# Attention, routed experts and a second MLP on one core: pairs of token groups taken in the order 2, 0, 1 in hidden quarters two to four, and the first pair's plain operands read where they lie

## The chip, the core and the metric

The kernel runs on one core of one Trainium2 chip. The metric is the device time of one execution in microseconds (us), as the median of several runs. The core has five engines with their own instruction queues, each of which runs its instructions in the order of the program: TensorE (PE, matmuls; PEld is its loading of weights), VectorE (DVE), ScalarE (ACT), GpSimd (POOL) and SyncE (SP, which here only starts transfers). An instruction may wait for another engine or for a transfer, and all that stands behind it in its queue then waits too. Matmuls read SBUF and write PSUM; a transfer that POOL starts goes through one queue, one that SP starts through another, and both move on the same 16 DMA engines.

## The reference, cut to what matters

```python
x = attention(q, k, v, omega)        # 4 x 8 heads x 576 tokens, random features; 2304 rows of 512
x = moe(x, w_gate, w1, w2)           # each row to one of 8 experts, 512 -> 1024 -> 512

def _moe2_ref(x, w_in, w_out):       # 2304 rows, 512 -> 2048 -> 512
    h = x @ w_in
    neg, pos = h <= -1, h >= 1
    g = np.where(pos, h, np.where(neg, 0.0, (h + 1) ** 2 / 4))
    return g @ w_out
```

The change lies in the last part, `_moe2_ref`, here called the second MLP.

## The kernel before

**Precision.** Every fp32 operand of a matmul is split into a high part (rounded) and a low part (the rest). One product is then three matmuls: high by high, high by low, low by high. So each operand, weights and activations alike, costs one rounding copy (on ACT) and one subtraction (on POOL or DVE).

**Second MLP, tiling.** The 2304 rows, transposed, lie in SBUF as `yT` (four tiles of 128 features). They are taken in six groups g of 384 rows; the groups 2p and 2p+1 are the pair p (0, 1, 2). The 2048 hidden features are taken in quarters qd of 512, four blocks f of 128 each.

Quarter 0 runs over groups with plain products. `z_h(u, fs)` makes two hidden blocks of group u (24 matmuls), `z_o(0, u, fs)` multiplies two of them by w_out (18 matmuls); the order of work for group u is z_h(u, blocks 0 and 1), z_o(0, u-1, blocks 2 and 3), z_h(u, blocks 2 and 3), z_o(0, u, blocks 0 and 1). The high and low parts of group u lie in `ys[u % 2]`, made by `z_split` one group ahead. After each hidden block DVE and ACT alternate: DVE clips the bank (`z_clip`), ACT squares, DVE takes a maximum (`z_g`), ACT rounds, DVE subtracts (`z_low`). ACT also copies finished output banks to `st` before the next z_o may use them.

Quarters 1 to 3 run over pairs with a 2 by 2 scheme of seven products instead of eight. `s_h(qd, p, a)` makes, for one half a of the quarter, four hidden blocks of a pair from seven products of 6 matmuls each (42 in all; here called a set). Product i multiplies a weight combination by operand i of the pair, which lies in DRAM as `yd[p][i]` (768 KB). Operands 0, 4 and 6 are plain parts of x, which `y_keep` stores from `ys`; 1, 2, 3 and 5 are differences, which the step stream "y" makes during quarter 0 (DVE subtracts, `y_round` rounds on ACT, subtracts on POOL and stores). `y_load(k)` fetches operand k of the running list (seven for each pair, three pairs for each quarter) into slot k modulo 9 of `yslots`, from POOL's queue; in the second half of each set, product i is followed by the fetch of list entry `k0 + 9 + i`. A set's first product goes to bank b1, from which ACT copies it (x1); the fifth product is then added into b1. The sets use a ring of five PSUM banks (`ps_h2`), the output products one of three (`ps_o`).

**The order of the side work** is written out by hand. Three step streams ("w": read, convert, combine and round the weights of the next quarter; "y": the differences; "z": `z_split` of the next group) are advanced by `tick`; in quarter 0 the table `BEAT` says after each third of a matmul block which stream goes on (z, y, w, or h for `y_round`). `gate` holds the weight stream back until the weights it overwrites are no longer needed. The nine slots are the two halves of `ys[0]`, five parts of a tile `yS` that takes the place of `yT` once that is no longer read, and the two halves of `ys[1]`.

Of the kernel before, what the change touches and what calls it, by code (L numbers as in the profile page):

```python
# [19 lines left out]
P = 128  # L20
# [6 lines left out]
G = 384  # L27
# [134 lines left out]
def kernel(  # L162
# [1102 lines left out]
    half_ys = [t[:, i * 4 * G:i * 4 * G + 4 * G] for t in ys for i in range(2)]  # L1265
    yslots = half_ys[0:2]

    def y_slots():
        flat = yp.tile([P, 3 * YW], F32R, name="yS", tag="yT")
        yslots.extend([flat[:, i * 4 * G:(i + 1) * 4 * G] for i in range(5)] + half_ys[2:4])  # L1270
        flat = yp.tile([P, YW], F32, name="yW", tag="yT3")
        wz[2:] = [flat[:, i * 512:i * 512 + 512] for i in range(2)]
        sts[0] = flat[:, 1024:1024 + TG * D]
    ends = range(NTILE - 2 * TG, NTILE)
    sts = [None, zp.tile([P, TG * D], F32, name="st1", tag="st1", bufs=1)]
# [33 lines left out]
    def z_g(ph, cl, key):  # L1309
        qd, g, f = key  # L1310
        gt = gs[g % 2][f + 4 * ((3 * qd + g // 2) % 2) if g % 2 and f < 2 else f]
        gtiles[key] = gt[:, 0], gt[:, 1]
        nc.vector.tensor_tensor(out=cl, in0=ph, in1=cl, op=ALU.max)  # L1313
        nc.scalar.activation(gt[:, 0], cl, AF.Copy)  # L1314
        return gt, cl
# [30 lines left out]
    def z_o(qd, g, fs):  # L1346
# [28 lines left out]
        if qd == 0:  # L1375
            nc.sync.dma_start(out=zd[g], in_=z_stage(qd, g))
        elif qd < 3:
            nc.gpsimd.dma_start(out=zd[g], in_=z_stage(qd, g), accum_op=ALU.add)
        elif g + 2 < NG:
            z_fetch(g + 2)  # L1380

# [28 lines left out]
    def y_stream():  # L1410
        for p in range(NG // 2):
            for s in range(2):
                b11, b12, b21, b22 = [yT[2 * i + s][:, (2 * p + j) * G:(2 * p + j) * G + G] for i in range(2) for j in range(2)]
                t1 = None
                for op in (3, 1, 5, 2):
                    yield "D"
                    hi, t, both = pair()
                    x, y = {3: (b12, b11), 2: (b22, b12), 1: (b22, t1), 5: (t1, b21)}[op]
                    nc.vector.tensor_sub(t, x, y)
                    if op in (3, 1):  # L1420
                        t1 = t
                    high.append((p, op, s, hi, t, both))

    def z_stream(u):
        for d in range(4):
            yield "A"
            z_split(u, d, nc.gpsimd)

# [3 lines left out]
    def beat(u):  # L1432
        n = count[u] + 3 * (u == 0 and count[u] > 7)
        count[u] += 1
        name = BEAT[n]
        if u == 0:
            name = name if n < 19 and name == "z" else "w" if n >= 19 else None
        elif u == NG - 1 and n < 11 and name == "y":
            name = "w"
        if name == "h":  # L1440
            y_round()
        elif name:
            tick(name)

    def y_load(k):
        q, op = divmod(k, 7)
        if q < 9:
            nc.gpsimd.dma_start(out=yslots[k % NSL], in_=yd[q % 3][op])


    def s_h(qd, p, a):
        k0 = 7 * (3 * (qd - 1) + p)
        b1, b2, b3, b4 = [ps_h2.tile([P, 512], F32, name="ph2", tag="ph2")[:, 0:G] for _ in range(4)]

# [13 lines left out]
        product(0, b1, True)  # L1468
        nc.scalar.activation(x1, b1, AF.Copy)
        tick("w")  # L1470
        product(1, b2, True)
        if a and p == 2:
            gate[0] = qd + 1
# [7 lines left out]
        tick("w", "A")  # L1481
        product(4, b1, False)
        q11 = z_clip(b1)
        product(5, b2, True)
        nc.vector.tensor_sub(x2, x2, b2)
        l11 = z_g(*q11, (qd, g0, f0))
        q21 = z_clip(x2)
        product(6, b4, False)
        nc.vector.tensor_add(x1, x1, b4)
        z_low(*l11)  # L1490
        q22 = z_clip(x3, x4)
# [9 lines left out]
    for u in range(NG):  # L1501
# [3 lines left out]
        else:  # L1505
# [3 lines left out]
            y_slots()  # L1509
            for k in range(2, 7):  # L1510
                y_load(k)
# [6 lines left out]
        if u < NG - 1:  # L1518
            drain("z")
        if u == NG - 2:  # L1520
            y_load(0)
            y_load(1)
        z_o(0, u, (0, 1))
# [3 lines left out]
    for qd in range(1, 4):  # L1527
        if qd == 3:
            z_fetch(0)
        for p in range(3):  # L1530
            s_h(qd, p, 0)
            if (qd, p) == (1, 0):
                z_o(0, g, (2, 3))
            else:
                z_o(qd - (p == 0), g, (0, 1))
                z_o(qd - (p == 0), g, (2, 3))
            if p == 0:
                gate[1] = qd + 1
            if (qd, p) == (3, 0):
                z_fetch(1)  # L1540
            s_h(qd, p, 1)
            if (qd, p) == (3, 2):
                flat = yp.tile([P, 3 * YW], F32, name="yF", tag="yT")
# [3 lines left out]
            z_o(qd, g, (0, 1))  # L1547
            if (qd, p) == (1, 0):
                tick("w")
                tick("w")  # L1550
# [6 lines left out]
    tot = nc.values_load(ints[0:1, 3, 0:1], min_val=0, max_val=8 * 16)  # L1557
    last = [z_stage(3, g)[:, j * D:j * D + D] for g in (NG - 2, NG - 1) for j in range(TG)]
    fw = [yT[j // 10][:, j % 10 * 256:j % 10 * 256 + 256] for j in range(16)]
# [108 lines left out]
```

## Time and profile before

| | |
|---|---|
| time, median of 3 runs | 799.04 us (798.63 to 799.64) |
| profiled execution, its own time | 803.65 us |
| its span, first to last instruction | 801.9 us |
| PE busy in the span | 754.3 us (94%) |
| DVE, ACT, POOL busy | 550.9, 392.7, 378.7 us |
| mean granted TensorE clock | 0.978 |

The span is what the profile shows of one execution. 1.75 us of that execution's time lie outside it, and it was 4.6 us longer than the median of the timed runs. The granted clock is the share of TensorE's full speed; 0.50 is the lower of its two levels. In the views below a time in brackets, as [2.53 <-DMA yS<-yd], is how long the engine was idle just before the row, and what ended that.

### The profile page before, as it was taken

The page shows a single profiled execution, that of the slowest core. Times are in us where ns is not written, and L with a number is a line of the kernel's source. Part 1 is how long each engine was busy: PE and PEld are TensorE (multiplying, and loading weights), DVE is VectorE, ACT ScalarE, POOL GpSimd, SP SyncE. Part 2 cuts the span into 40 slices and gives each one's busy share as a digit, 9 for nine tenths or more (in the row PEclk, how much of TensorE's full clock was granted, in tenths as well). Part 3 has the DMA queues.
Part 4 walks back from the last instruction along what each step waited for, and adds up shares of the span by engine and source line. Part 5 has one row for each costly group of instructions (what it writes and reads, how often), then busy time and mean ns, then how long its engine had stood idle before and what let it go on. Part 6 is the DMA issues. An engine that isn't in the chain of part 4 may idle for free. (4 is left out here: it accounts for less than half of the span.)

```text
span 801.9 us, 17043 instructions
## 1 busy us (share of the span) xinstructions
PE 754.3 (94%) x6428; PEld 690.5 (86%) x6428; DVE 550.9 (69%) x1170; ACT 392.7 (49%) x973; POOL 378.7 (47%) x429
## 2 busy tenths in 40 slices
PE   6898899588999999999999999799999999999997
PEld 4787788558999999999989889589899889988985
DVE  3678787945756775565778887677656866676663
ACT  5999799522422222222356754354554554552230
POOL 5658851535455545523747876143145233432312
PEclk9999999888999999999999999799999999999999
DMA  9977301164566766655446588796987986968822
GB/s 220 228 162 220 94 30 29 72 181 158 174 198 196 216 183 219 211 171 159 132 140 263 236 318 295 297 384 168 314 273 190 376 247 196 358 195 306 307 112 83
DMA packets 94236, 166.61 MB, mean 208 GB/s; under 512 B 28528, under 2 KB 61424, under 8 KB 94144
## 3 DMA queue, kind: packets, MB, share of 16 engines
q1 hardware_dynamic: 79136, 93.91, 37.4%
q0 software_dynamic: 14112, 69.80, 26.8%
q10 hardware_dynamic: 896, 1.70, 0.6%
q8 instruction: 53, 0.87, 0.4%
q14 instruction: 39, 0.32, 0.1%
HBM read 125.29 MB, written 40.11 MB: 206 GB/s over the span
## 5 line engine op out<-in xcount | busy, mean ns | idle before, releaser
L278 POOL TENSOR_SCALAR wh<-wraw 128x1024 fp32r<-128x1024 f32 x60 | 73.1, 1219 | 106.7 <-DMA wraw<-in_moe_w_dram 69.0
L1357 PE MATMUL po<-wl,g 128*128 128x512 f32 x288 | 114.2, 397 | 1.4 <-POOL wl L300 1.4
L1356 PE MATMUL po<-wh,g 128*128 128x512 f32 x288 | 114.3, 397 | 1.3 <-ACT st L1362 1.3
L1358 PE MATMUL po<-wh,g 128*128 128x512 f32 x288 | 114.2, 396 | 0.0
L390 DVE TENSOR_TENSOR wl<-wraw,wh 128x1024 fp32r<-128x1024 f32 x60 | 85.3, 1430 | 9.5 <-POOL wh L278 9.5
L300 POOL TENSOR_TENSOR wl<-wz,wh 128x256 fp32r<-128x256 f32 (+1 forms) x43 | 40.4, 945 | 97.6 <-ACT wh L314 97.6
L616 ACT ACTIVATE pp<-ps,bi 128x128 f32<-128x128 f32 x288 | 84.5, 481 | 3.1 <-DVE bi L612 3.1
L1306 ACT ACTIVATE cl<-cl,half 128x384 f32<-128x384 f32 x78 | 47.4, 609 | 72.8 <-DVE cl L1305 72.8
L1156 PE MATMUL ph<-xh,wh 128*128 128x288 f32 (+6 forms) x256 | 77.9, 304 | 4.2 <-DVE hl L1162 3.8
L1157 PE MATMUL ph<-xl,wh 128*128 128x288 f32 (+6 forms) x256 | 77.7, 304 | 0.1
L1158 PE MATMUL ph<-xh,wl 128*128 128x288 f32 (+6 forms) x256 | 77.6, 303 | 0.0
L1174 PE MATMUL py<-hh,wh 128*128 128x288 f32 (+6 forms) x256 | 77.6, 303 | 0.0
L1176 PE MATMUL py<-hh,wl 128*128 128x288 f32 (+6 forms) x256 | 76.5, 299 | 0.0
L1175 PE MATMUL py<-hl,wh 128*128 128x288 f32 (+6 forms) x256 | 76.4, 298 | 0.0
L1357 PEld LDWEIGHTS po<-wl,g 128*128 128x128 f32 x288 | 54.5, 189 | 13.5 <-POOL wl L300 1.9
L1356 PEld LDWEIGHTS po<-wh,g 128*128 128x128 f32 x288 | 54.7, 190 | 13.1 <-ACT st L1362 1.6
L1358 PEld LDWEIGHTS po<-wh,g 128*128 128x128 f32 x288 | 54.5, 189 | 12.8
L1161 ACT ACTIVATE hh<-ph 128x288 fp32r<-128x288 f32 (+6 forms) x64 | 26.8, 418 | 76.3 <-PE ph L1158 74.1
L1318 DVE TENSOR_TENSOR g<-cl,g 128x384 fp32r<-128x384 f32 x78 | 48.3, 619 | 22.4 <-ACT g L1314 22.4
L1162 DVE SCALAR_TENSOR_TENSOR hl<-ph,hh 128x288 fp32r<-128x288 f32 (+6 forms) x64 | 29.1, 461 | 49.7 <-ACT hh L1161 49.6
L1314 ACT ACTIVATE g<-cl 128x384 fp32r<-128x384 f32 x78 | 40.5, 520 | 34.0 <-DVE cl L1313 33.9
L605 DVE TENSOR_REDUCE nsq<-ps 128x4 f32<-128x512 f32 x72 | 46.9, 683 | 11.5 <-PE ps L600 11.4
(218 smaller groups left out, 2078.0 us busy)
## 6 DMA issues: line engine op xcount, KB each, us to landing
wraw<-in_moe_w_dram SPq DMA_DIRECT2D x57, 512.0 KB, 4.0
yS<-yd POOLq DMA_DIRECT2D x35, 768.0 KB, 12.1
ys<-yd POOLq DMA_DIRECT2D x28, 768.0 KB, 12.5
yd<-tt SPq DMA_DIRECT2D x24, 384.0 KB, 2.6
wraw<-in_moe_w_in_dram SPq DMA_DIRECT2D x16, 512.0 KB, 6.7
wraw<-in_moe_w_out_dram SPq DMA_DIRECT2D x16, 512.0 KB, 8.2
yd<-ys SPq DMA_DIRECT2D x9, 768.0 KB, 5.3
zd<-st SPq DMA_DIRECT2D x6, 768.0 KB, 4.4
```

The lines of the kernel that those rows point to most:

```text
L278: nc.gpsimd.tensor_scalar(out=hi, in0=t, scalar1=1.0, scalar2=1.0, op0=ALU.mult, op1=ALU.mult)
L390: nc.vector.tensor_sub(lo, t, hi.bitcast(F32))
L616: act.activation(at(ppb)[:, 2 * j + i, :], at(pjb[i])[:, j, :], AF.Exp, bias=r["bi"][:, j, i:i + 1])
L1156: nc.tensor.matmul(ph, lhsT=wh[:, d, c], rhs=xh, start=(d == 0), stop=False)
L1157: nc.tensor.matmul(ph, lhsT=wh[:, d, c], rhs=xl, start=False, stop=False)
L1158: nc.tensor.matmul(ph, lhsT=wl[:, d, c], rhs=xh, start=False, stop=(d == 3))
L1174: nc.tensor.matmul(py, lhsT=wh[:, a, c], rhs=hh, start=(f == 0), stop=False)
L1175: nc.tensor.matmul(py, lhsT=wh[:, a, c], rhs=hl, start=False, stop=False)
L1176: nc.tensor.matmul(py, lhsT=wl[:, a, c], rhs=hh, start=False, stop=(f == 7))
L1356: nc.tensor.matmul(po, lhsT=gh[:, c], rhs=wh, start=(f == 0), stop=False)
L1357: nc.tensor.matmul(po, lhsT=gh[:, c], rhs=wl, start=False, stop=False)
L1358: nc.tensor.matmul(po, lhsT=gl[:, c], rhs=wh, start=False, stop=(f == 3))
```

## The change

Five things change together. Pairs are taken in the order 2, 0, 1 in quarters 1 to 3, and by the stream "y". The first nine slots are arranged so that the plain operands 0, 4 and 6 of pair 2 are read from `ys`, where groups 4 and 5 still lie; no transfer fetches them. In the two halves of that first set the products run in the order 0, 6, 4, 1, 2, 3, 5, product 6 into a fifth bank of its own that DVE adds later. `z_split` subtracts on DVE for the first two of its four parts, where POOL did all. In group 0 the weight stream gets two ticks that were empty.

```diff
-    yslots = half_ys[0:2]
+    ORDER = (2, 0, 1)
+    yslots = []
 
     def y_slots():
         flat = yp.tile([P, 3 * YW], F32R, name="yS", tag="yT")
-        yslots.extend([flat[:, i * 4 * G:(i + 1) * 4 * G] for i in range(5)] + half_ys[2:4])
+        part = [flat[:, i * 4 * G:(i + 1) * 4 * G] for i in range(5)]
+        yslots.extend([half_ys[0], part[0], part[1], part[2], half_ys[1], part[3], half_ys[3], part[4], half_ys[2]])
...
     def y_stream():
-        for p in range(NG // 2):
+        for p in ORDER:
...
         for d in range(4):
             yield "A"
-            z_split(u, d, nc.gpsimd)
+            z_split(u, d, nc.vector if d < 2 else nc.gpsimd)
...
         if u == 0:
-            name = name if n < 19 and name == "z" else "w" if n >= 19 else None
+            name = "w" if n >= 19 else name if name == "z" or (name == "w" and n > 10) else None
...
     def s_h(qd, p, a):
-        k0 = 7 * (3 * (qd - 1) + p)
-        b1, b2, b3, b4 = [ps_h2.tile([P, 512], F32, name="ph2", tag="ph2")[:, 0:G] for _ in range(4)]
+        k0 = 7 * (3 * (qd - 1) + ORDER.index(p))
+        b1, b2, b3, b4, *b5 = [ps_h2.tile([P, 512], F32, name="ph2", tag="ph2")[:, 0:G] for _ in range(4 + (k0 == 0))]
...
         nc.scalar.activation(x1, b1, AF.Copy)
+        if b5:
+            product(6, b5[0], True)
+            product(4, b1, False)
+            q11 = z_clip(b1)
         tick("w")
...
-        product(4, b1, False)
-        q11 = z_clip(b1)
+        if not b5:
+            product(4, b1, False)
+            q11 = z_clip(b1)
         product(5, b2, True)
...
-        product(6, b4, False)
+        if not b5:
+            product(6, b4, False)
         nc.vector.tensor_add(x1, x1, b4)
+        if b5:
+            nc.vector.tensor_add(x1, x1, b5[0])
...
             y_slots()
-            for k in range(2, 7):
+            for k in (1, 2, 3, 5):
                 y_load(k)
...
-        if u == NG - 2:
-            y_load(0)
-            y_load(1)
```

The loops over pairs, the fetches of `zd` and the two groups that are stored last follow `ORDER`, and the list entries after the ninth are fetched in the order of the products that free their slots.

On POOL's queue, at the end of group 5's first hidden blocks, this stood before (`tt` are differences, `wl` low parts of weights, `yd` the operands):

```order
L1403 TENSOR_TENSOR tt_6674<-tt_6674 128x384 [waits DMAHW7_49,DVE_49]
L1448 DMA ys0_3147<-yd00_74 128x1536 [waits DMAHW5_49,PE_49]
L1448 DMA ys0_3147<-yd01_75 128x1536 [waits DMAHW6_49,PE_49]
L1403 TENSOR_TENSOR tt_6698<-tt_6698 128x384 [waits DMAHW0_49,Activation_49]
L1403 TENSOR_TENSOR tt_6737<-tt_6737 128x384 [waits DMAHW1_49,Activation_49]
L1448 DMA yS_6751<-yd02_76 128x1536 [waits Pool_49]
L1448 DMA yS_6751<-yd03_77 128x1536
L1448 DMA yS_6751<-yd04_78 128x1536
L1448 DMA yS_6751<-yd05_79 128x1536
```

and this stands there now:

```order
L1406 TENSOR_TENSOR tt_6677<-tt_6677 128x384 [waits DMAHW7_49,DVE_49]
L300 TENSOR_TENSOR wl4_3127<-wz0_3140,wh4_3126 128x256 [waits Activation_49]
L1406 TENSOR_TENSOR tt_6700<-tt_6700 128x384 [waits DMAHW0_49,Activation_49]
L1406 TENSOR_TENSOR tt_6738<-tt_6738 128x384 [waits DMAHW1_49,Activation_49]
L1451 DMA yS_6752<-yd21_89 128x1536 [waits Pool_49]
L1451 DMA yS_6752<-yd22_90 128x1536
L1451 DMA yS_6752<-yd23_91 128x1536
L1451 DMA yS_6752<-yd25_93 128x1536
```

Seven fetches ahead of the first set (a fifth into `yS`, yd06, follows the rows shown) became four, and the two into `ys0` that stood first are gone.

On ACT's queue, between the two halves of the first set, this stood before (`st` is the output stage, `wx` and `wh` a weight's conversion and rounding, L1469 the copy x1 of the second half):

```order
L1314 ACTIVATE g14_5937<-cl_6975 128x384 [waits DVE_49]
L1362 ACTIVATE st1_5928<-po_6874 128x512 [waits DMAHW0_49,PE_49]
L252 ACTIVATE wx_6995<-wraw_6838 128x512 [waits DMAHW1_49,Activation_49]
L1362 ACTIVATE st1_5928<-po_6875 128x512 [waits PE_49]
L1362 ACTIVATE st1_5928<-po_6876 128x512 [waits PE_49]
L314 ACTIVATE wh0_112<-yW_6752 128x512 [waits DVE_49]
L1469 ACTIVATE tt_7021<-ph2_7017 128x384 [waits DMAHW5_49,PE_49,Pool_49]
```

and this now (the copy is L1472):

```order
L1317 ACTIVATE g14_5937<-cl_6981 128x384 [waits DVE_49]
L1365 ACTIVATE st1_5928<-po_6879 128x512 [waits DMAHW1_49,PE_49]
L1365 ACTIVATE st1_5928<-po_6880 128x512 [waits PE_49]
L314 ACTIVATE wh0_112<-yW_6753 128x512 [waits DVE_49]
L1365 ACTIVATE st1_5928<-po_6881 128x512 [waits PE_49]
L252 ACTIVATE wx_7018<-wraw_6844 128x512 [waits DMAHW2_49,Activation_49]
L1472 ACTIVATE tt_7028<-ph2_7023 128x384 [waits DMAHW5_49,PE_49,Pool_49]
```

Both times the copy stands behind a rounding of weights (`wh0<-yW`) that waits for DVE; now an output copy and a conversion stand between the two. On PE the product that must wait for this copy has moved from fifth to third place.

On DVE's queue the rows that follow the last product of the first half were these before (L1485 to L1318 finish the four hidden blocks, L253 to L257 convert a weight for the rounding above):

```order
L1489 TENSOR_TENSOR tt_6907<-tt_6907,ph2_6906 128x384 [waits PE_49]
L1318 TENSOR_TENSOR g00_5929<-cl_6948,g00_5929 128x384 [waits Activation_49]
L1305 TENSOR_SCALAR tt_6908<-tt_6908 128x384
L1313 TENSOR_TENSOR cl_6960<-tt_6907,cl_6960 128x384 [waits Activation_49]
L1305 TENSOR_SCALAR cl_6975<-tt_6907 128x384 [waits DVE_49]
L1318 TENSOR_TENSOR g01_5930<-cl_6960,g01_5930 128x384 [waits Activation_49]
L1313 TENSOR_TENSOR tt_6908<-tt_6908 128x384
...
L253 TENSOR_SCALAR wy_6996<-wraw_6838 128x512 [waits DMAHW1_49]
L255 SCALAR_TENSOR_TENSOR wy_6996<-wx_6995,wy_6996 128x512 [waits DVE_49,Activation_49]
L257 SCALAR_TENSOR_TENSOR yW_6752<-wraw_6838,wy_6996 128x512 [waits DVE_49]
```

and are these now:

```order
L1493 TENSOR_TENSOR tt_6908<-tt_6908,ph2_6904 128x384 [waits DVE_49,PE_49]
L1316 TENSOR_TENSOR cl_6929<-ph2_6903,cl_6929 128x384 [waits Activation_49]
L1308 TENSOR_SCALAR cl_6971<-tt_6908 128x384 [waits DVE_49]
L1498 TENSOR_TENSOR tt_6908<-tt_6908,ph2_6906 128x384
L1500 TENSOR_TENSOR tt_6908<-tt_6908,ph2_6907 128x384 [waits DVE_49]
L1321 TENSOR_TENSOR g00_5929<-cl_6929,g00_5929 128x384 [waits Activation_49]
L1308 TENSOR_SCALAR tt_6909<-tt_6909 128x384
...
L1321 TENSOR_TENSOR g14_5937<-cl_6981,g14_5937 128x384 [waits Activation_49]
L255 SCALAR_TENSOR_TENSOR wy_6944<-wx_6943,wy_6944 128x512
L257 SCALAR_TENSOR_TENSOR yW_6753<-wraw_6809,wy_6944 128x512 [waits DVE_49]
```

Before, 13 rows stand from the first to the last of these, now 16: the set ends with product 5, so the subtraction, a maximum, a clip and the added bank now stand behind it, and the conversion's first row (L253) has moved ahead of it.

## Rows read from the trace of the kernel before

**Rows 1.** Waits of PE from 395 to 802 us: total, times, longest.

```profile
PE ph L1460 <- DMA yS<-yd: 4.4, 2, 2.5
PE ph L1460 <- DVE cl L1305: 1.5, 1, 1.5
PE po L1357 <- POOL wl L300: 1.4, 1, 1.4
PE po L1356 <- ACT st L1362: 1.3, 1, 1.3
```

**Rows 2.** Windows: length, each engine's busy us, granted PE clock, DMA share, GB/s.

```profile
498.10:514.10 16.00, 10.15 (x44) 8.90 (x44) 7.88 (x14) 5.19 (x10) 3.13 (x3) 0.76 1.07 411
...
536.00:551.70 15.70, 15.70 (x79) 14.13 (x78) 11.50 (x24) 8.00 (x17) 4.09 (x6) 1.00 0.73 233
...
567.40:796.00 228.60, 228.52 (x1129) 204.31 (x1127) 149.02 (x305) 99.68 (x197) 73.33 (x98) 1.00 0.75 245
```

**Rows 3.** Timeline of PE at the first set: start, us, then the instruction.

```profile
498.15 0.34 PE L1460 MATMUL ph<-ys,wh 128*128 128x384 f32 x1
498.33 0.34 PE L1461 MATMUL ph<-ys,wh 128*128 128x384 f32 x1
...
512.02 0.66 PE L1460 MATMUL ph<-yS,wh 128*128 128x384 f32 x1 [1.46 <-DVE cl L1305]
...
516.64 0.40 PE L1356 MATMUL po<-wh,g 128*128 128x512 f32 x1
...
527.63 0.39 PE L1356 MATMUL po<-wh,g 128*128 128x512 f32 x1
```

**Rows 4.** Timeline of POOL: the fetches ahead of the first set.

```profile
484.85 1.19 POOL L1448 DMA_DIRECT2D ys<-yd  x2
...
489.44 2.69 POOL L1448 DMA_DIRECT2D yS<-yd  x5
```

**Rows 5.** Landing: the second yS fetch alone, issued at 489.99; then all five.

```profile
yS<-yd POOLq DMA_DIRECT2D x1, 768.0 KB, 11.2
DMA to landing us min/median/max: 8.9/14.5/20.3
```

**Rows 6.** Timeline of ACT: the copies x1 (L1469) of the first set's halves.

```profile
501.12 0.48 ACT L1469 ACTIVATE tt<-ph 128x384 f32<-128x384 f32 x1
...
521.34 0.63 ACT L314 ACTIVATE wh<-yW 128x512 fp32r<-128x512 f32 x1 [0.51 <-DVE yW L257]
521.88 0.47 ACT L1469 ACTIVATE tt<-ph 128x384 f32<-128x384 f32 x1
```

**Rows 7.** Timeline of DVE after the last product of the first half.

```profile
514.32 0.55 DVE L1489 TENSOR_TENSOR tt<-tt,ph 128x384 f32<-128x384 f32 x1 [2.43 <-PE ph L1462]
514.79 0.55 DVE L1318 TENSOR_TENSOR g<-cl,g 128x384 fp32r<-128x384 f32 x1
...
520.62 0.69 DVE L257 SCALAR_TENSOR_TENSOR yW<-wraw,wy 128x512 int32<-128x512 int32 x1
```

**Rows 8.** Timeline of DVE, then of PE, around group 4's first hidden blocks.

```profile
472.76 0.55 DVE L1305 TENSOR_SCALAR cl<-ph 128x384 f32<-128x384 f32 x1
...
466.76 0.33 PE L1329 MATMUL ph<-ys,wl 128*128 128x384 f32 x1
...
476.79 0.50 PE L1356 MATMUL po<-wh,g 128*128 128x512 f32 x1 [1.27 <-ACT st L1362]
```

**Rows 9.** Groups by line: POOL and DVE from 397.8 to 498.1, DVE from 536 to 779.

```profile
L1078 POOL TENSOR_TENSOR ys<-yT,ys 128x384 fp32r<-128x384 f32 x20 | 23.6, 1180 | 15.9 <-ACT ys L1077 15.7 <-PE ph L1329 0.2
...
L1318 DVE TENSOR_TENSOR g<-cl,g 128x384 fp32r<-128x384 f32 x22 | 17.2, 784 | 14.5 <-ACT g L1314 14.5
...
L1318 DVE TENSOR_TENSOR g<-cl,g 128x384 fp32r<-128x384 f32 x45 | 24.9, 554 | 5.4 <-ACT g L1314 5.4
```

**Rows 10.** PE after an earlier wait for DVE; window after it, columns as in rows 2.

```profile
183.28 0.61 PE L1156 MATMUL ph<-xh,wh 128*128 128x288 f32 x1 [3.49 <-DVE hl L1162]
...
182.20:188.90 6.70, 5.62 (x23) 5.62 (x24) 4.59 (x7) 1.00 (x2) 2.61 (x2) 0.50 0.50 157
```

More of the change, by code (lines that the diff above doesn't have):

```diff
@@ L1273, in y_slots @@
         sts[0] = flat[:, 1024:1024 + TG * D]
-    ends = range(NTILE - 2 * TG, NTILE)
+    ends = range(2 * ORDER[2] * TG, 2 * ORDER[2] * TG + 2 * TG)
+    follow = {2 * p + i: 2 * ORDER[n + 1] + i for n, p in enumerate(ORDER[:2]) for i in range(2)}
     sts = [None, zp.tile([P, TG * D], F32, name="st1", tag="st1", bufs=1)]
@@ L1310, in z_g @@
         qd, g, f = key
-        gt = gs[g % 2][f + 4 * ((3 * qd + g // 2) % 2) if g % 2 and f < 2 else f]
+        gt = gs[g % 2][f + 4 * ((3 * qd + (ORDER.index(g // 2) if qd else g // 2)) % 2) if g % 2 and f < 2 else f]
         gtiles[key] = gt[:, 0], gt[:, 1]
@@ L1378, in z_o @@
             nc.gpsimd.dma_start(out=zd[g], in_=z_stage(qd, g), accum_op=ALU.add)
-        elif g + 2 < NG:
-            z_fetch(g + 2)
+        elif g in follow:
+            z_fetch(follow[g])
     def z_stage(qd, g):
@@ L1447, in y_load @@
         if q < 9:
-            nc.gpsimd.dma_start(out=yslots[k % NSL], in_=yd[q % 3][op])
+            nc.gpsimd.dma_start(out=yslots[k % NSL], in_=yd[ORDER[q % 3]][op])
     def s_h(qd, p, a):
-        k0 = 7 * (3 * (qd - 1) + p)
-        b1, b2, b3, b4 = [ps_h2.tile([P, 512], F32, name="ph2", tag="ph2")[:, 0:G] for _ in range(4)]
+        k0 = 7 * (3 * (qd - 1) + ORDER.index(p))
+        b1, b2, b3, b4, *b5 = [ps_h2.tile([P, 512], F32, name="ph2", tag="ph2")[:, 0:G] for _ in range(4 + (k0 == 0))]
         def product(i, bank, first):
@@ L1469, in s_h @@
         nc.scalar.activation(x1, b1, AF.Copy)
+        if b5:
+            product(6, b5[0], True)
+            product(4, b1, False)
+            q11 = z_clip(b1)
         tick("w")
         product(1, b2, True)
-        if a and p == 2:
+        if a and p == ORDER[2]:
             gate[0] = qd + 1
@@ L1528 @@
         if qd == 3:
-            z_fetch(0)
-        for p in range(3):
+            z_fetch(2 * ORDER[0])
+        for n, p in enumerate(ORDER):
             s_h(qd, p, 0)
-            if (qd, p) == (1, 0):
+            if (qd, n) == (1, 0):
                 z_o(0, g, (2, 3))
             else:
-                z_o(qd - (p == 0), g, (0, 1))
-                z_o(qd - (p == 0), g, (2, 3))
-            if p == 0:
+                z_o(qd - (n == 0), g, (0, 1))
+                z_o(qd - (n == 0), g, (2, 3))
+            if n == 0:
                 gate[1] = qd + 1
-            if (qd, p) == (3, 0):
-                z_fetch(1)
+            if (qd, n) == (3, 0):
+                z_fetch(2 * ORDER[0] + 1)
             s_h(qd, p, 1)
-            if (qd, p) == (3, 2):
+            if (qd, n) == (3, 2):
                 flat = yp.tile([P, 3 * YW], F32, name="yF", tag="yT")
@@ L1547 @@
             z_o(qd, g, (0, 1))
-            if (qd, p) == (1, 0):
+            if (qd, n) == (1, 0):
                 tick("w")
@@ L1557 @@
     tot = nc.values_load(ints[0:1, 3, 0:1], min_val=0, max_val=8 * 16)
-    last = [z_stage(3, g)[:, j * D:j * D + D] for g in (NG - 2, NG - 1) for j in range(TG)]
+    last = [z_stage(3, g)[:, j * D:j * D + D] for g in range(2) for j in range(TG)]
     fw = [yT[j // 10][:, j % 10 * 256:j % 10 * 256 + 256] for j in range(16)]
```

## The prediction

> **What bounds the kernel now.** I read the waits of PE first, since PE is busy 94% of the span. From 395 us on they fit into four rows [rows 1]: 5.9 us inside one set of products (4.4 for fetched operands, and 1.5 that the view puts down to DVE), and two single waits in quarter 0, 1.4 us for a weight's low part and 1.3 us for an output copy. The windows then show where PE can't be improved [rows 2]: from 536 to 551.7, a set and 36 output matmuls, it is busy all of 15.7 us, and from 567.4 to 796 it misses 0.1 of 228.6 us. There the matmuls themselves are the limit; the change leaves their number as it is.
>
> What is left is the first half of the first set, which opens at 498.15 [rows 3]. Matmuls follow each other there every 0.18 us (498.15 to 498.33); I use 0.175, so 42 take 7.35 us. A set and 36 output matmuls take 15.7 [rows 2], so the 36 take 8.35 and 18 take 4.2. First half, 18 output matmuls and second half would be 18.9 us at full speed. The trace shows 498.15 to 527.63 [rows 3], 29.5 us: 10.6 too many. 5.9 are the waits. Most of the rest is the clock: in 498.1 to 514.1 the granted share is 0.76 [rows 2], and full speed is back at 516.64, where a matmul takes 0.40 again [rows 3].
>
> The waits are for transfers, the third too. Five fetches into yS start from 489.44 on [rows 4] and land 8.9 to 20.3 us after their issue [rows 5]. The last was issued about 0.5 us before POOL was done at 492.13 [rows 4], so it landed near 511.9; product 6 starts at 512.02 [rows 3], and the DVE instruction that the row names is not what it waited for.
>
> **The change, part by part.**
>
> *Fetches.* Before, two fetches into ys stood ahead in POOL's queue, from 484.85 on [rows 4], so the fourth in that queue was the second into yS: issued at 489.99, landed 11.2 later, at 501.2 [rows 5]. Now the last operand that the set needs is itself the fourth, its queue starting up to 4.6 us later (489.44 against 484.85). It lands between 501.2 and 505.8. Product 5, which reads it, is last in the new order, due 6.3 us after 498.15 without any wait, and at 505.8 by the sum below. So the fetches cost nothing any more, 1.3 us at worst if nothing else delayed PE; what covers them is the three products that read ys.
>
> *The copy x1, first half.* The price of the new order is that product 4, which adds into b1, is third instead of fifth, and must wait for ACT's copy of b1. Before, that copy ended at 501.60 [rows 6], 3.45 us after the set began, ahead of the fifth product. Products 0 and 6 take 2.1. If ACT is as late as before, PE waits 1.35 us. One more weight conversion now stands ahead on DVE, and two fetches no longer do on POOL; bounds 0 and 2.7. The five remaining products end at 3.45 + 5.25 = 8.7.
>
> *The copy x1, second half.* The output matmuls end at 12.9, products 0 and 6 at 15.0. The copy stands on ACT behind the rounding of a weight that waits for DVE, and DVE reaches that weight only after finishing the first half. Before, this chain ran from 514.32 to 521.31, 13 rows in 7.0 us [rows 7]. Now it has 16 rows; three more at the 0.47 us from row to row (514.32 to 514.79) make 8.4. ACT's rounding and the copy took 521.34 to 522.35, 1.0 us [rows 6]; two more rows at the 0.54 from start to start there make 2.1. So the copy ends at 8.7 + 8.4 + 2.1 = 19.2, and PE, due at 15.0, waits 4.2 us. Before, the fifth place hid this: PE reached it 4.2 us after the second half began. Bounds 0 and 5.7 (POOL now issues fetches in that stretch).
>
> *The clock.* A wait of 3.49 us earlier in this execution was followed by a stretch at 0.50, 182.2 to 188.9 [rows 10], of which PE worked 5.6 us (from 183.28); at full speed that is 2.8 us less work. I take 2.8 for the new wait too; bounds 0 and 5.
>
> The second half then ends at 19.2 + 5.25 + 2.8 = 27.2 instead of 29.5: a gain of 2.3 us. Bounds: 10.6 if both waits are hidden; a loss of 2.5 if both have their upper bound (1.35 and 1.5 more) and the clock costs 5.
>
> *Two ticks in group 0.* The weight that PE waited 1.4 us for starts two ticks sooner. A tick is at least a matmul triple, 0.53 us, and weight ticks in a hidden block are four of these apart, so two are 2 us or more: the wait goes. Gain 1.4, bounds 0 and 1.4.
>
> *z_split on DVE.* Ten subtractions move (two in each of five groups). On POOL one takes 1.18 us; a subtraction of the same form on DVE takes 0.55 where POOL is little used and 0.78 in quarter 0 [rows 9]. So POOL loses 2.4 us for each group and DVE gains 1.1 to 1.6, to which waits for ACT's rounding copy just ahead may come. That matters because DVE is late in group 4: PE's last hidden matmul there ends at 467.09, DVE's clip of that bank starts at 472.76, 5.7 us after [rows 8]; from that clip over ACT to the output copy is 4.0 us, at 476.79, while PE was free 1.27 us sooner. So lateness above 4.4 us becomes a wait, one for one. Against the added work stand less interference from POOL (0.78 back towards 0.55 on these rows) and one conversion fewer between groups 1 and 4, as the weights run ahead. I take 0.3 us of further wait; bounds -1.3 (the wait goes) and +4.
>
> *The rest.* The other order of pairs changes only which data move. The fetches for the second pair are issued in another order (entries 9, 15, 13, 10, 11, 12, 14), while PE still has some 16 us of other work ahead of them; cost nothing, at worst one wait of 1 to 2 us. The fifth bank leaves no spare one between the halves, but DVE frees b1 and the fifth bank within 2.5 us of the last product, inside the 4.2 us of output matmuls.
>
> **Sum.** -2.3 - 1.4 + 0.3 = -3.4 us. On the profiled execution's own time 803.65 becomes 800.2 (its span 801.9 becomes 798.5). The runs' median is 4.6 lower than that execution; I carry the difference over, 799.04 - 3.4 = 795.6. A measurement of this kernel tells about 0.2%, 1.6 us, from no change.
>
> **Rivals.**
>
> *The waits go and nothing takes their place.* If DVE is ahead by then (it idles while PE waits elsewhere) or ACT's copy is early, the set runs near full speed: with one short wait and no loss of clock, gain 6 to 9 us, so 790 to 793. Against it: the order on ACT is fixed, and the chain behind the second copy is counted from rows.
>
> *Everything is given back at the second copy.* With 5.7 us of wait and the clock down until far into the next output matmuls, only the 1.4 us remain or less: 797.5 to 800.6, no change. The trace has such a long low stretch: from within the set's waits to 516.64 [rows 3].
>
> *Slower: DVE becomes the bound of quarter 0.* A moved subtraction has to wait for ACT's rounding copy, which stands behind another (about 1 us), and for POOL. With 1.0 us of such wait and 0.78 of work for each, 3.6 us for each group, DVE is some 7 us later at group 4 after two saturated groups; the wait there grows from 1.3 to above 7, which eats all of the gain: 801 to 803. It decides from about 3.4 us of added wait on. For it: the 5.7 us; against it: POOL's 2.4 us less. The Trainium skill speaks for this one: by SBUF — State Buffer, section Who interferes with whom, a DVE instruction with two SBUF inputs and a GpSimd instruction that reads SBUF shut each other out for a whole instruction. The trace agrees in kind, with 0.78 against 0.55 us on such rows [rows 9]. In Perfetto Trace Analysis, section Optimizing Scalar/DVE Operations, the skill adds that moving work between these two engines might not help.
>
> *The fetches are still late.* If the four fetches share the DMA engines worse than counted and the last lands at 508 or later, PE waits again in the first half, 2 us or more, and the whole gain shrinks to about 1 us: 798.
>
> **Chances.** The forecast, with -1.6 to -6 us: 0.50. Waits gone: 0.18. All given back: 0.14. Slower by DVE: 0.13. Fetches late: 0.05. Faster by over 0.2%: the first two and a little of the others, 0.68; within 0.2%: 0.18; slower: 0.14. The range leaves out the best part of the second case and the worst of the fourth: 791.0 to 800.5; the forecast's own is 793.0 to 797.4.
>
> **What would show it.** The change in place: no PE wait for DMA between 498 and 512, the row of a wait for ACT (tt, the copy) of about 1.3 us in the first half and of about 4 us in the second, and a granted clock below 1 after that. No wait for a low part of weights near 415. In group 4 a wait for the output copy near 1.5 us, DVE's clips 4 to 7 us behind PE. From the second pair on PE without a gap. The prediction is wrong if the second half shows no wait for ACT (then it is faster), or if the waits in groups 2 to 5 sum to over 4 us (then slower).

## The result, and the profile after

The changed kernel takes 810.9 us (median of six runs, 809.41 to 813.34); the kernel before, run beside it, takes 799.48 (six runs). The ratio is 1.0144, its 95% interval 1.0119 to 1.0168: 9.5 to 13.4 us slower, where 3.4 us less were forecast and the range ended at 800.5.

The profiled execution of after takes 810.58 us, its span is 808.5. The spans of the two profiles differ by 6.6 us and the medians by 11.4. Of the 4.8 us between these two figures, 2.3 lie ahead of everything that the change touches: before's two profiles reached the first group's first matmul at 397.83 and 398.79 us, after's at 395.52, the other eleven of this study at 391.8 to 394.5, with the same instructions up to there. So profiles are compared below from that matmul on.

First the waits of PE in after, from 395 to 810 us, the view of [rows 1]:

```profile
PE po L1359 <- ACT st L1365: 8.4, 4, 3.1
PE ph L1463 <- ACT tt L1472: 4.3, 2, 4.1
```

Three of the four rows of before are gone: no wait for fetched operands, none for the low part of a weight. In their place the wait for an output copy, 1.3 us once in before, is 8.4 us in four pieces. Next the windows of after, columns as in [rows 2]:

```profile
395.52:505.33 109.81, 101.41 (x487) 89.75 (x487) 84.45 (x137) 62.02 (x131) 58.87 (x57) 0.97 0.63 235
458.90:466.70 7.80, 6.04 (x20) 4.82 (x21) 7.18 (x11) 5.34 (x11) 4.05 (x4) 0.78 0.36 140
478.90:488.70 9.80, 6.65 (x25) 5.21 (x24) 7.73 (x15) 7.41 (x16) 5.83 (x6) 0.83 0.69 273
505.33:530.10 24.77, 20.68 (x104) 19.56 (x103) 14.66 (x29) 10.78 (x21) 7.54 (x9) 0.93 0.72 261
538.50:798.80 260.30, 260.13 (x1285) 232.53 (x1283) 172.66 (x351) 116.12 (x230) 82.47 (x112) 1.00 0.75 245
```

The first window is the group stage, from the first group's first matmul to the first set: 109.8 us. In before it was 397.83 to 498.15 [rows 3], 100.3. The fourth is the first set, 24.8 us where before had 29.5 [rows 3]. From the second pair on PE is busy throughout, as in [rows 2]. The second and third windows lie around the two longest waits, and show the granted clock down to 0.78 and 0.83. PE's timeline has the four waits and the first set:

```profile
422.77 0.50 PE L1359 MATMUL po<-wh,g 128*128 128x512 f32 x1 [1.82 <-ACT st L1365]
441.73 0.50 PE L1359 MATMUL po<-wh,g 128*128 128x512 f32 x1 [1.61 <-ACT st L1365]
460.66 0.50 PE L1359 MATMUL po<-wh,g 128*128 128x512 f32 x1 [1.82 <-ACT st L1365]
...
482.76 0.80 PE L1359 MATMUL po<-wh,g 128*128 128x512 f32 x1 [3.15 <-ACT st L1365]
...
505.33 0.34 PE L1463 MATMUL ph<-ys,wh 128*128 128x384 f32 x1
523.21 0.45 PE L1463 MATMUL ph<-ys,wh 128*128 128x384 f32 x1 [4.09 <-ACT tt L1472]
...
530.10 0.39 PE L1359 MATMUL po<-wh,g 128*128 128x512 f32 x1
```

The group stage has 5.7 us more of waiting than before (8.4 against 1.4 and 1.3 [rows 1]). Most of the other 3.8 of its 9.5 us more are matmuls at half clock behind the third and fourth wait: the second window, 7.8 us at a granted clock of 0.78, and the third, 9.8 us at 0.83, lose 1.7 us each. The row at 482.76 already shows it, with 0.80 us where the first ones behind the other waits take 0.50.

Why the output copies are late stands in VectorE's timeline in group 1 (the wait at 422.77 is this group's), and in ScalarE's beside it:

```profile
414.37 0.55 DVE L1308 TENSOR_SCALAR cl<-ph 128x384 f32<-128x384 f32 x1
416.02 0.56 DVE L1078 TENSOR_TENSOR ys<-yT,ys 128x384 fp32r<-128x384 f32 x1 [1.10 <-ACT ys L1077]
416.50 0.56 DVE L1422 TENSOR_TENSOR tt<-yT,tt 128x384 f32<-128x384 f32 x1
...
419.00 0.55 DVE L1308 TENSOR_SCALAR cl<-ph 128x384 f32<-128x384 f32 x1
```

```profile
414.96 0.62 ACT L1309 ACTIVATE cl<-cl,half 128x384 f32<-128x384 f32 x1 [0.28 <-DVE cl L1308]
415.48 0.51 ACT L1077 ACTIVATE ys<-yT 128x384 fp32r<-128x384 f32 x1
...
421.71 0.52 ACT L1317 ACTIVATE g<-cl 128x384 fp32r<-128x384 f32 x1 [1.09 <-DVE cl L1316]
422.14 0.58 ACT L1365 ACTIVATE st<-po 128x512 f32<-128x512 f32 x1
```

The row at 416.02 is a moved subtraction. It needs ScalarE's rounding copy of 415.48, which stands behind the square of 414.96, which needs VectorE's own clip of 414.37. So the subtraction waits for a round trip that began with the instruction ahead of it on its own engine: 1.10 us of idle and 0.56 of work. The next clip, at 419.00, is late by both. ScalarE's work on that clip ends with the row at 421.71, which waits for VectorE; right behind it stands the output copy at 422.14, and PE goes on at 422.77. Summed over the stage, VectorE's row in the waits of all engines, 395 to 505 us:

```profile
DVE ys L1078 <- ACT ys L1077: 7.6, 8, 1.1
```

Last, the end of the program: GpSimd's last store, and the span.

```profile
799.85 0.96 POOL L1392 DMA_INDIRECT out_dram<-st,oidx  x1 [0.44 <-DVE st L1367]
```

```profile
core 0: 808.5 us, clock 0.978
```

From the end of that row, 800.81, to the end of the span are 7.7 us. The same stretch of before is 4.0 us in its first profile and 3.7 in its second (below). No step of the prediction had that.

### The profile page after: what moved, and what is told of

Same layout as the page of the kernel before. It is cut to its first block, busy times and chain, and to the rows that moved or that the text cites. A ratio compares the mean times of both kernels' runs of the same rounds, so it can differ in the third digit from the quotient of the medians.

```text
span 808.5 us, 17041 instructions
## 1 busy us (share of the span) xinstructions
PE 755.5 (93%) x6428; PEld 691.1 (85%) x6428; DVE 550.2 (68%) x1182; ACT 393.7 (49%) x973; POOL 363.5 (45%) x416
## 5 line engine op out<-in xcount | busy, mean ns | idle before, releaser
L278 POOL TENSOR_SCALAR wh<-wraw 128x1024 fp32r<-128x1024 f32 x60 | 70.0, 1170 | 106.3 <-DMA wraw<-in_moe_w_dram 77.9
L1359 PEld LDWEIGHTS po<-wh,g 128*128 128x128 f32 x288 | 54.9, 191 | 21.6 <-ACT st L1365 9.7
L1162 DVE SCALAR_TENSOR_TENSOR hl<-ph,hh 128x288 fp32r<-128x288 f32 (+6 forms) x64 | 29.2, 462 | 51.9 <-ACT hh L1161 51.7
L1321 DVE TENSOR_TENSOR g<-cl,g 128x384 fp32r<-128x384 f32 x78 | 45.8, 587 | 22.9 <-ACT g L1317 22.9
```

The costliest lines, as they stand in the source:

```text
L278: nc.gpsimd.tensor_scalar(out=hi, in0=t, scalar1=1.0, scalar2=1.0, op0=ALU.mult, op1=ALU.mult)
L1359: nc.tensor.matmul(po, lhsT=gh[:, c], rhs=wh, start=(f == 0), stop=False)
```

## The experiments

For each profile the time from the first group's first matmul on is split at three matmuls: the first of the first set, the first behind its second half, and the end of the last one. In us, with the last column the number of transfers that GpSimd issues (counted in the traces):

| kernel | group stage | first set | rest | behind last matmul | sum | transfers |
|---|---|---|---|---|---|---|
| before | 100.3 | 29.5 | 268.3 | 5.9 | 404.0 | 117 |
| before_again | 100.3 | 29.1 | 268.3 | 5.7 | 403.3 | 117 |
| after | 109.8 | 24.8 | 268.8 | 9.6 | 413.0 | 114 |
| after_split_gpsimd | 102.0 | 27.5 | 268.8 | 9.8 | 408.1 | 114 |
| before_split_dve | 109.7 | 28.1 | 268.3 | 5.6 | 411.8 | 117 |
| after_split_later | 103.9 | 27.1 | 268.8 | 9.6 | 409.3 | 114 |
| before_ticks | 102.7 | 27.8 | 268.3 | 5.6 | 404.4 | 117 |
| gpsimd_no_ticks | 100.2 | 24.9 | 268.8 | 10.2 | 404.2 | 114 |
| second_half_order | 100.2 | 21.8 | 269.4 | 10.0 | 401.3 | 114 |
| second_half_117 | 100.2 | 21.6 | 269.3 | 6.1 | 397.3 | 117 |
| three_fetches_by_sync | 100.2 | 29.1 | 268.3 | 10.0 | 407.5 | 114 |
| one_fetch_by_sync | 100.2 | 29.3 | 268.3 | 6.6 | 404.4 | 116 |
| six_fetches_by_sync | 100.2 | 29.2 | 269.6 | 9.4 | 408.4 | 111 |
| three_more_on_gpsimd | 100.2 | 30.0 | 268.3 | 5.4 | 403.9 | 120 |

**after_split_gpsimd**: the moved subtractions back on GpSimd.

```
-            z_split(u, d, nc.vector if d < 2 else nc.gpsimd)
+            z_split(u, d, nc.gpsimd)
```

> The changed kernel with one part undone: all subtractions of z_split on GpSimd again, nothing else differs from after. Theory A (the ten moved subtractions make VectorE late in quarter 0, and what is lost there is their doing): the four waits of PE for the output copy, 8.4 us in after, shrink to 2 us or less, the stretch from the first group's first matmul to the first set's is again about 100 us (100.3 before, 109.8 after), and the time is 793 to 801 us: before's 799.5 less the 4.7 us that the first set gained in after's trace and the 1.4 us of the low part of weights is 793.4; 797 if the 3.65 us that after's program takes longer behind PE's last matmul belong to the change, 801 if nothing but the group stage comes back. Rival B (the weight stream, two ticks ahead, has moved VectorE's work so that it is late): the waits stay above 6 us and the time above 806 us.

Measured: 803.45 us, ratio to before 1.0042 (1.0022 to 1.0062). The group stage is 102.0 us, and the waits of PE from 391 us on read:

```profile
PE ph L1463 <- ACT tt L1472: 5.6, 3, 4.1
PE ph L1331 <- POOL ys L1078: 1.7, 2, 1.1
...
PE po L1359 <- ACT st L1365: 0.5, 1, 0.5
```

8.4 us of waits for the output copy are 0.5. Theory A holds: 7.8 of the 9.5 us are the moved subtractions'. The time is above the 793 to 801 expected: the group stage keeps 1.7 us, the end its 4, and the first set has 2.7 us more than in after.

**before_split_dve**: the same part alone, in the kernel before.

```
-            z_split(u, d, nc.gpsimd)
+            z_split(u, d, nc.vector if d < 2 else nc.gpsimd)
```

> The kernel before with this one part of the change alone: the subtractions of z_split for d below 2 on VectorE, in groups 1 to 5. Theory A: the group stage grows by 7 to 11 us, as in after, with waits of PE for the output copy of more than 6 us in sum, and the time is 806 to 811 us. Rival B (the ticks are what makes VectorE late, or the two parts do so only together): within 2 us of before, 798 to 802 us.

Measured: 808.34 us, ratio 1.0113 (1.0086 to 1.014), 7.9 us above the 800.46 of before beside it. Waits of PE and of VectorE in the group stage:

```profile
DVE ys L1078 <- ACT ys L1077: 8.9, 9, 1.1
PE po L1356 <- ACT st L1362: 8.6, 4, 3.9
```

Without the ticks, the order and the operands in place, the same two rows appear with much the same sizes, and the group stage grows by 9.4 us. Rival B falls.

**after_split_later**: same work on VectorE, each subtraction one step of the stream after its rounding copy.

```
+            if 0 < d < 3:
+                nc.vector.tensor_sub(y_part(u, d - 1, 1), yT[d - 1][:, c], y_part(u, d - 1, 0).bitcast(F32))
+            if d < 2:
+                nc.scalar.activation(y_part(u, d, 0), yT[d][:, c], AF.Copy)
+            else:
+                z_split(u, d, nc.gpsimd)
-            z_split(u, d, nc.vector if d < 2 else nc.gpsimd)
```

> The changed kernel, with the ten moved subtractions still on VectorE but each one step of the stream later: a step of the stream issues the rounding copy of its own part on ScalarE and the subtraction of the part before, so that VectorE finds that copy long done. The work on VectorE and the number of its instructions are those of after. Theory A1 (what makes VectorE late is its wait for the rounding copy right ahead, 7.6 us in eight waits in after's trace): these waits go, the waits of PE for the output copy fall below 4 us, the time is 799 to 804 us. Rival A2 (it is the work itself, with what GpSimd and VectorE take from each other at SBUF): VectorE is as late as in after, the time stays within 2 us of after, 808 to 812 us.

Measured: 805.71 us, ratio 1.0086 (1.0052 to 1.012). The place in group 1, on VectorE's timeline (the moved subtraction is L1432 here), and from the group stage the waits of PE and the row of the ten moved subtractions:

```profile
412.90 0.55 DVE L1308 TENSOR_SCALAR cl<-ph 128x384 f32<-128x384 f32 x1
413.37 0.55 DVE L1432 TENSOR_TENSOR ys<-yT,ys 128x384 fp32r<-128x384 f32 x1
...
416.33 0.55 DVE L1308 TENSOR_SCALAR cl<-ph 128x384 f32<-128x384 f32 x1
```

```profile
PE po L1359 <- ACT st L1365: 2.4, 4, 1.1
```

```profile
L1432 DVE TENSOR_TENSOR ys<-yT,ys 128x384 fp32r<-128x384 f32 x10 | 8.7, 869 | 0.1
```

The subtraction follows its clip without idle time, all ten together waited 0.1 us, and from clip to clip are 3.4 us instead of 4.6. The group stage is 103.9 us. Of the 7.8 us between 102.0 and 109.8, the wait for the rounding copy is 5.9, the work itself 1.9. A1 holds in the rows, as far as three kernels tell the two apart; the time is 1.7 us above what it named.

**before_again**: the kernel before, once more.

> The kernel before, unchanged, for a second profile of it. Its first profiled execution took 803.65 us, 4.2 more than the median of its runs. What every theory expects: about 799 us, waits of PE in quarter 0 of 1.4 and 1.3 us and of 5.9 us in the first set. Open, and read from it: whether the 100.3 us of the group stage and the 6.0 us from PE's last matmul to the end repeat, or which stretch was long in the first profile. If the stretch behind PE's last matmul varies by some 4 us without any change, then the 3.65 us more in after's trace are not the change's doing.

Measured: 803.96 us in this execution, with the group stage 100.3 and the end 5.7 us as in the first profile; it is 5 us above the 799 expected, and reached the group stage at 398.79, later than any other profile. The end does not vary by 4 us in these two, which speaks for after's longer end being the change's. Its last store and span:

```profile
797.44 0.96 POOL L1389 DMA_INDIRECT out_dram<-st,oidx  x1 [0.44 <-DVE st L1364]
```

```profile
core 0: 802.1 us, clock 0.977
```

**before_ticks**: the two ticks alone, in the kernel before.

```
-            name = name if n < 19 and name == "z" else "w" if n >= 19 else None
+            name = "w" if n >= 19 else name if name == "z" or (name == "w" and n > 10) else None
```

> The kernel before with the two extra weight ticks in group 0 alone. The prediction's term: the wait of 1.4 us for a weight's low part goes and nothing takes its place, 1.4 us less than before. Rival (the conversions then stand in VectorE's queue ahead of the clips of groups 1 to 3, VectorE gets later by 1 to 2 us there, and new short waits appear in groups 1 to 4): group stage 101 to 103 us, time 1 to 2 us above before.

Measured: 800.04 us, ratio 1.0002 (0.9984 to 1.0021): nothing. PE's waits from 393 to 500 us:

```profile
PE ph L1328 <- POOL ys L1078: 1.7, 2, 1.1
PE po L1356 <- ACT st L1362: 0.5, 1, 0.5
PE ph L1327 <- ACT ys L1077: 0.5, 1, 0.5
```

The wait for the low part is gone, as forecast, and the one of 1.3 us for the output copy is 0.5. In their place stand waits for token parts from GpSimd and ScalarE. The group stage is 2.4 us longer, as the rival has it, the first set 1.3 to 1.7 shorter, and the time is as neither has it.

**gpsimd_no_ticks**: after_split_gpsimd without the ticks.

```
-            name = "w" if n >= 19 else name if name == "z" or (name == "w" and n > 10) else None
+            name = name if n < 19 and name == "z" else "w" if n >= 19 else None
```

> after_split_gpsimd with the two extra weight ticks of group 0 taken out as well: what is left of the change is the order of pairs, the first set's operands read from the token tiles, and the order of its products. Theory (each part's worth adds): group stage 100 to 101 us with the waits of 1.4 and 1.3 us of before back, where after_split_gpsimd had 102.0; first set 27 to 28 us as there; the end 9.7 us as there; so 801 to 802.5 us, 1 to 2 less than after_split_gpsimd: the ticks cost instead of gaining 1.4. Rival (the ticks do gain 1.4, and what made the group stage of after_split_gpsimd longer is the other order of the token differences): group stage 102 us or more, time 803.5 to 806 us.

Measured: 802.05 us, ratio 1.0021 (1.0004 to 1.0038). PE's waits from 393 us on:

```profile
PE ph L1463 <- ACT tt L1472: 3.8, 2, 3.6
PE po L1360 <- POOL wl L300: 1.4, 1, 1.4
PE po L1359 <- ACT st L1365: 1.2, 1, 1.2
```

The group stage is that of before, so the other order of token differences costs it nothing. The stages sum to 3.9 us less than in after_split_gpsimd, the medians differ by 1.4 with intervals that overlap: that the ticks cost something here is likely, its size open. The first set is shorter than expected, 24.9 us: the first half's wait for the copy, 1.3 us in after_split_gpsimd, is gone.

**second_half_order**: product 4 in its old place in the second half.

```
         if b5:
             product(6, b5[0], True)
+        if b5 and not a:
             product(4, b1, False)
             q11 = z_clip(b1)
...
-        if not b5:
+        if a or not b5:
             product(4, b1, False)
             q11 = z_clip(b1)
```

> gpsimd_no_ticks with one more edit: in the second half of the first set, product 4 stands in its old place, behind product 3, while product 6 stays second; the first half keeps the changed order. Theory (the 4.1 us for the copy x1 in the second half, and the half clock behind it, are what the early place of product 4 costs): no wait over 1 us in the second half, the first set 20.5 to 22 us instead of 27.5, the time 5 to 7 us below gpsimd_no_ticks, 795 to 797 us. Rival (VectorE's chain behind the copy is late in any case, and the wait only moves to a later product): a wait of 2 to 4 us stands there at another product, the time within 2 us of gpsimd_no_ticks.

Measured: 797.64 us, ratio 0.9968 (0.9946 to 0.9991), 4.4 us below gpsimd_no_ticks. The first set is 21.8 us. Its waits are the same as in second_half_117 below: 1.4 for VectorE (tt L1483) and 0.9 for the copy. So part of the wait did move to a later product, as the rival has it (1.4 us, where the theory had none over 1 us), and the larger part is gone, as the theory has it: the first set lies in its range, the time 0.6 us above.

**three_fetches_by_sync**: the kernel before, three transfers moved from GpSimd to SyncE.

```
+            if k < 60:
                 nc.gpsimd.dma_start(out=yslots[k % NSL], in_=yd[q % 3][op])
+            else:
+                nc.sync.dma_start(out=yslots[k % NSL].bitcast(F32), in_=yd[q % 3][op])
```

> The kernel before, with the last three fetches of operands (entries 60, 61 and 62, in quarter 3) issued by SyncE instead of GpSimd, so that GpSimd issues 114 transfers as in after, and not 117. It asks why the stretch behind PE's last matmul, in which GpSimd issues the last stores and then drains its queue, is 9.6 to 9.8 us in each kernel with the change and 5.6 to 5.9 us in each without. Theory T1 (the length of GpSimd's closing drain goes with the number of transfers that it issued): 9 to 10 us behind the last matmul, time 3 to 4.5 us above before, 803 to 805 us. Rival T2 (it goes with what is stored last, the groups 2 and 3 in place of 4 and 5, or with the place of the code): 5.5 to 6 us, time as before, 799 to 801 us.

Measured: 803.33 us, ratio 1.0047 (1.0025 to 1.0069). Everything up to PE's last matmul is as in before, and the end has grown by 4 us:

```profile
791.39 0.96 POOL L1389 DMA_INDIRECT out_dram<-st,oidx  x1 [0.44 <-DVE st L1364]
```

```profile
core 0: 800.4 us, clock 0.976
```

From the end of the last store (792.35) to the end are 8.05 us, against 3.7 in before_again. What is stored last, and the order of pairs, are those of before. T1 holds, T2 falls.

**second_half_117**: second_half_order with three fetches of `zd` on GpSimd, 117 transfers again (`zd`, in DRAM, holds the output sums of each group; a fetch of it is 768 KB, as one of an operand).

```
-        nc.sync.dma_start(out=z_stage(3, g), in_=zd[g])
+        (nc.gpsimd if g < 3 else nc.sync).dma_start(out=z_stage(3, g), in_=zd[g])
```

> second_half_order, with three of the six fetches of zd in quarter 3 (groups 0, 1 and 2) issued by GpSimd instead of SyncE, so that GpSimd issues 117 transfers again, as in before, and not 114. Theory T1 (GpSimd's closing drain is 4 us longer with 114 transfers than with 117, whatever they carry): 5.6 to 6.0 us behind PE's last matmul instead of 9.98, and 4 us less time than second_half_order, 793 to 794.5 us, faster than both kernels. Rival T3 (not the number counts but that the last transfers of operands on GpSimd come earlier, or what is stored last): the end stays at 9.5 to 10 us and the time within 1.5 us of second_half_order.

Measured: 794.49 us, ratio 0.9921 (0.9892 to 0.9949): faster than both kernels. Its last store, its span, and PE's waits from 393 us on:

```profile
785.23 0.96 POOL L1392 DMA_INDIRECT out_dram<-st,oidx  x1 [0.44 <-DVE st L1367]
```

```profile
core 0: 790.4 us, clock 0.987
```

```profile
PE po L1360 <- POOL wl L300: 1.4, 1, 1.4
PE ph L1463 <- DVE tt L1483: 1.4, 1, 1.4
PE po L1359 <- ACT st L1365: 1.2, 1, 1.2
PE ph L1463 <- ACT tt L1472: 0.9, 2, 0.5
```

The end is back: 4.2 us behind the last store, though the transfers that were added are of another kind than the ones taken away. T3 falls. The time is 3.1 us below that of second_half_order, where 4 were expected.

**one_fetch_by_sync, six_fetches_by_sync, three_more_on_gpsimd**: the kernel before with 116, 111 and 120 transfers. The first two have the edit of three_fetches_by_sync with 62 and 57 for 60, the third has that of second_half_117 with g > 2.

> The kernel before with one fetch of operands (entry 62) issued by SyncE, so that GpSimd issues 116 transfers. If the closing drain grows with each transfer that is missing, the stretch behind PE's last matmul is 6.9 to 7.3 us (a third of the 4 us); if it is one step that comes somewhere between 114 and 117, it is 5.7 or 9.8 us.

> The kernel before with six fetches of operands (entries 57 to 62) issued by SyncE: GpSimd issues 111 transfers. If the closing drain grows with each transfer that is missing, the stretch behind PE's last matmul is about 13.5 to 14 us; if it is one step, 9.8 us as with 114; if it comes and goes with the number, it can be 5.7 us again.

> The kernel before with three fetches of zd in quarter 3 (groups 3, 4 and 5) issued by GpSimd instead of SyncE: GpSimd issues 120 transfers. If the closing drain shortens with each transfer, the stretch behind PE's last matmul is 1.5 to 2.5 us; if it is one step below 117, it stays at 5.6 to 5.9 us; if it comes and goes with the number, it can be 9.8 us.

Measured, one profile each, behind the last matmul: 6.6 us with 116, 9.4 with 111, 5.4 with 120. With the others: 5.4 to 6.6 us from 116 transfers up, 9.4 to 10.2 from 114 down. The 6.6 lies between the forecasts, but its last stores came later; from the last store to the end it has 4.2 us, as second_half_117. So these counts show a step of about 4 us between 116 and 114, not a price for each transfer. Only transfers of 768 KB were added or taken away, so the number is not told apart from the bytes.

## Why the prediction was wrong, step by step

**The step that failed is the one on z_split**: "I take 0.3 us of further wait; bounds -1.3 (the wait goes) and +4". In the group stage it measured 7.8 us (after against after_split_gpsimd), and 9.4 us alone (before_split_dve against before); by the medians of the time, 7.5 and 7.9. The step charged VectorE 0.55 to 0.78 us for each subtraction, mentioned that waits for the rounding copy "may come", and set GpSimd's relief against both. The relief is real: VectorE's subtractions L1321 take 663 ns on average in after, as the lines of the group stage show, where before had 784 [rows 9]; before_split_dve has 667, after_split_later 736. By the Trainium skill (SBUF — State Buffer, section Who interferes with whom) these and GpSimd's reads exclude each other, and the trace agrees with that direction. But ports decide little here: the work with all its interference is 1.9 us, the wait 5.9.

```profile
L1321 DVE TENSOR_TENSOR g<-cl,g 128x384 fp32r<-128x384 f32 x23 | 15.3, 663 | 15.7 <-ACT g L1317 15.7
...
L1078 DVE TENSOR_TENSOR ys<-yT,ys 128x384 fp32r<-128x384 f32 x12 | 8.5, 722 | 7.6 <-ACT ys L1077 7.6
```

The wait that the step left without a number is the round trip shown above: of the eight waits, seven are 1.0 to 1.1 us (four begin with a clip, three with a difference of tokens that VectorE has just made), one is 0.2. With the work of the moved subtractions (0.56 to 1.06 us each) that is 3.4, 3.7 and 3.4 us in groups 2, 3 and 4, against 3.6 for each group in the rival "DVE becomes the bound of quarter 0". The rival was right about the wait and its size, its chance of 0.13 too low, and its 801 to 803 too small: it gave the lateness back once, at group 4. PE gave it back in four places, in groups 1 to 4, and behind two of them the clock fell too. The waits in groups 2 to 4 sum to 6.6 us, above the 4 that the prediction named as the sign of this case.

The idle time of the old engine does not give this price. GpSimd's 20 subtractions waited 15.7 us for their rounding copies before [rows 9], and the ten that it kept wait nearly as long in after. In the group stage of before and of after:

```profile
POOL ys L1078 <- ACT ys L1077: 15.7, 8, 5.1
```

```profile
POOL ys L1078 <- ACT ys L1077: 13.9, 4, 5.3
```

They are a few long waits of an engine with time to spare, up to 5 us each, where VectorE's are short ones that begin with its own instruction just ahead.

**The two ticks** were to gain 1.4 us. The wait that they aimed at went, and others came: nothing by itself (1.0002), and the group stage of after_split_gpsimd 1.8 us longer than that of gpsimd_no_ticks. The step never asked what is queued behind two more conversions, and the one on z_split even counted them as a relief.

**The end** was in no step. Reading three operands in place removes three transfers of GpSimd's, and that lengthens the program's end by 3.8 us. "Fetches cost nothing any more" is true of PE's waits only.

**What held.** No wait for a fetch is left in the first set. The copy in the second half was forecast to cost 4.2 us and costs 4.09; the clock behind it 2.8, measured 1.6 (523.21 to 530.10 is 6.9 us for the five products behind the wait, which take 5.25 at full speed). The first half's wait, 1.35, is 1.3 in the two kernels with the ticks and a faster group stage, and none in after or in gpsimd_no_ticks. So the first set gained 4.5 us on the mean of before's two profiles, 2.3 forecast; in after_split_gpsimd, where the first half's wait does stand, it gained 1.8. The bound of the loss there should read 2.7 instead of 2.5 (1.35, 1.5 and 2.2 more, less 2.3); nothing hangs on it. The reading that before's third wait was for a transfer too is borne out: the second profile puts 4.7 us in three waits down to DMA. From the second pair on PE is solid; that stretch costs 0.5 us, nothing forecast, and why stays open.

By stages: 7.8 + 1.8 - 4.5 + 0.5 + 3.8 = 9.4 us, against 9.3 between the sums of after and of before's two profiles (413.0 less 403.7), and 9.5 to 13.4 between the timed runs. Some 2 us of the 11.4 between the medians are not placed in a stage.

## What to carry to other kernels

When an instruction changes engine, look at what its producer waits for. If the producer stands behind work that itself waits for the new engine, the moved instruction costs that engine a round trip besides its own work, here 1.0 to 1.1 us each time, and all that stands behind it in the queue is late by that too. The idle column of the old engine's row warns that there is a wait, but does not give its size. Moving the consumer one step later in the stream took three quarters of that price away without moving any work. And look at the whole program's end when transfers are added or removed, not only at who waits for them.

## What the hardware did that was not expected

The time from GpSimd's last store to the program's end is 3.5 to 4.2 us in kernels in which GpSimd issues 116 to 120 transfers, and 7.4 to 8.3 us with 111 or 114, though the last store lands some 3 us after its issue in both. Two ways of getting to 114 and two of getting to 117 agree. The longer time is in one instruction, the DRAIN with which GpSimd ends its work; in these lines of before and of after (shortest, median and longest of three, in ns) it is the longest:

```profile
L1663 POOLq DRAIN  x3: 46/112/3932, 796.7 to 801.6; - x3
```

```profile
L1671 POOLq DRAIN  x3: 46/113/7999, 799.6 to 808.2; - x3
```

It takes 3.6 to 4.1 us in the seven profiles with 116 transfers or more, and 7.8 to 8.3 us in the seven with 114 or 111. What it does in that time the trace does not show, and 115 was not run.

In code that the change does not touch, one wait near 180 us differs from profile to profile: 3.49 us in before [rows 10], and on PE's timeline of after and of after_split_gpsimd

```profile
181.99 0.46 PE L1156 MATMUL ph<-xh,wh 128*128 128x288 f32 x1 [2.13 <-DVE hl L1162]
```

```profile
179.51 0.40 PE L1156 MATMUL ph<-xh,wh 128*128 128x288 f32 x1 [0.18 <-DVE hl L1162]
```

Between before and after_split_gpsimd this wait (3.3 us more) and the clock behind it (2.8 us by [rows 10], none in after_split_gpsimd) make up the 6.0 us by which they reach the group stage apart. It is not the only such place: before's second profile waits 2.4 us there and is later still. So a difference of spans of 5 us says nothing here unless the stage is known in which it arose.
